# Short matmuls set between long ones in a TensorE-bound attention and gMLP kernel, and a last output tile cut 384 + 128

## The chip, the cores and the metric

The kernel runs on one core of a Trainium2 chip. The metric is the device time of one execution in microseconds; the time of a version is the median over its runs. Five engines work side by side, each through its own list of instructions in order: TensorE (PE; its weight loads are shown apart as PEld), VectorE (DVE), ScalarE (ACT), GpSimd (POOL) and SyncE (SP), which here only issues transfers.

## The reference

Two branches share the input x of 2048 rows by 512 columns, and a sigmoid gate per row mixes them.

```python
g = sigmoid((x * gate_w).sum(-1, keepdims=True))
# a: linear attention, 32 heads of 16
q, k, v = split(x @ wqkv)
phi(p) = concat(softmax(p @ w_phi), softmax(-(p @ w_phi)))      # 32 features per head
kv = einsum('bhsf,bhsd->bhfd', phi(k), v);  z = phi(k).sum over s
a = ((phi(q) @ kv) / (phi(q) . z + 1e-6)) @ wo
# b: gMLP
h = gelu(x @ w_in)                                              # 512 -> 1376
z1, z2 = h[:, :688], layernorm(h[:, 688:])
b = (z1 * (w_sp @ z2 + b_sp)) @ w_out                           # w_sp is 2048 x 2048
out = g * a + (1 - g) * b
```

All inputs are bfloat16. The product `w_sp @ z2` mixes along the rows and is the largest piece of work.

## The kernel before

Rows are cut into 16 tiles of 128. The order on each engine is written out by hand: the sequence in which the Python code calls its helpers is the sequence on every engine. All sums lie in one PSUM tile `ps` with 8 banks of 512 columns.

First come, per row tile, the input product of the gMLP (`z_piece`, L180), GELU on ACT, layer norm on DVE, and the value product (`v_proj`, L282). In between, `fold` multiplies the feature map into the key and query weights.

Then the loop at L516 runs 16 steps. Each step i has

- a spatial half tile `gg_half` (L396): 16 products of 344 columns that accumulate in bank 0 or 1. Two half tiles make one row tile of `w_sp @ z2`. When a half is done, DVE computes `u` from it (L404); after the second half, SP issues the transpose of `u` and the load of the spatial weights eight tiles on;
- `k_norm(i)`: DVE sums (L338) and inverts (L340), and then scales half of the key features, groups 0 to 3, while GpSimd scales groups 4 to 7 (L342);
- `kv_acc(i - 2)` (L372), the key sums: eight products of 65 columns, one per group of four heads, with a weight load each. They accumulate over all tiles in banks 3 and 4, called `slots`;
- `k_proj(i + 2)`: four products of 512 columns (L327), then two exponentials on ACT (L333). In three of the steps a query tile is projected, and another half tile and the query's `q_norm` follow.

Two more half tiles, the key sums of tiles 14 and 15 and `kv_extract` (DVE, L379 and L384) stand between this loop and the next.

The loop at L535 runs 16 steps j over the query tiles. Eleven half tiles are left; `gg_at` says which steps have one (step 2 has two, and steps 4, 6, 8, 10, 12 and 15 none). Each step has these half tiles, then `q_num(j)`: the query sums, eight products of 68 columns into `slots` (L420), which need the transposed query features of the tile (a transfer issued by `q_norm` three steps before, L364) and the release of `slots` by DVE, which reads them in `rd` (L424) and `o` (L426); SP then issues the transpose of `o` (L433). Then `q_proj(j + 4)`, `q_norm(j + 3)` and `out_tile(j - 3)`: 6 products for the gMLP (L439) and 4 for the attention (L444), a copy by ACT (L448) and the store (L449). The last output tile, 15, is made in two parts of 256 columns in banks 6 and 7, the first stored from SP's queue, the second from ACT's.

Of the kernel before, what the change touches and what calls it, by code (L numbers as in the profile page):

```python
# [14 lines left out]
P = 128  # L15
S = 2048
D = 512
# [5 lines left out]
NT = S // P  # L23
NDT = D // P
# [6 lines left out]
NHG = 8  # L31
HW = 4 * DH
VP = HW + 2
QW = HW + 4
# [5 lines left out]
def kernel(  # L40
# [14 lines left out]
    nc = tc.nc  # L55
# [9 lines left out]
    ps = psp.tile([P, 8, CH], FP32, name="ps")  # L65
# [5 lines left out]
    xT = pers.tile([P, NDT, S], BF16, name="xT")  # L71
    w_in = pers.tile([P, NDT, F + 1], BF16, name="w_in")
    wv = pers.tile([P, NDT, D], BF16, name="wv")
    wq = pers.tile([P, NDT, D], BF16, name="wq")
    wk = pers.tile([P, NDT, D], BF16, name="wk")
# [4 lines left out]
    vv = pers.tile([P, NT, NHG, VP], BF16, name="vv")  # L80
    wsp = pers.tile([P, WSLOTS, NT, P], BF16, name="wsp")
    kvx = pers.tile([P, NHG, QW], BF16, name="kvx")
# [59 lines left out]
    def load_wsp(t):  # L142
        nc.sync.dma_start_transpose(
            out=wsp[:, t % WSLOTS, :, :], in_=B_w_sp[t * P:(t + 1) * P, :]
        )
# [166 lines left out]
    KBANK = (2, 6)  # L312
    QBANK = (5, 7)
    ek_t = {}
    eq_t = {}
    w_in_flat = w_in[:].rearrange("p d f -> p (d f)")

    def e_slot(i):
        if i == 5:
            flat = xn[:].rearrange("p t d -> p (t d)")  # L320
        else:
            flat = w_in_flat[:, i * 2 * D:(i + 1) * 2 * D]
        return flat.rearrange("p (g a n) -> p g a n", g=NHG, a=2)

    def feat(t, w, b, e):
        for dt in range(NDT):
            nc.tensor.matmul(  # L327
                ps[:, b, :], lhsT=xT[:, dt, t * P:(t + 1) * P], rhs=w[:, dt, :],
                start=(dt == 0), stop=(dt == NDT - 1),
            )  # L330
        src = ps[:, b, :].rearrange("p (g n) -> p g n", g=NHG)
        for a, sc in enumerate((1.0, -1.0)):
            nc.scalar.activation(out=e[:, :, a, :], in_=src, func=AF.Exp, scale=sc)  # L333
# [12 lines left out]

    def k_proj(t):
        ek_t[t] = e_slot(t % 4)
        feat(t, wk, KBANK[t % 2], ek_t[t])

    def k_norm(t):
        norm(ek_t[t])

    def q_proj(t):
        eq_t[t] = e_slot(4 + t % 2 if t < 4 else (t - 4) % 6)
        feat(t, wq, QBANK[t % 2], eq_t[t])

    eT_t = {}

    def q_norm(t):  # L360
        e = eq_t.pop(t)
        norm(e)
        eT = wqkT[:, 2 * (t % 4):2 * (t % 4) + 2, :].rearrange("p a (b n) -> p (a b) n", n=P)
        nc.sync.dma_start_transpose(out=eT, in_=e.rearrange("p g a n -> p (g a n)"))  # L364
        eT_t[t] = eT

    slots = ps[:, 3:5, :].rearrange("p b (c w) -> p (b c) w", w=P)

    def kv_acc(t):
        ek = ek_t.pop(t)  # L370
        for g in range(NHG):
            nc.tensor.matmul(  # L372
                slots[:, g, 0:HW + 1], lhsT=ek[:, g, :, :].rearrange("p a n -> p (a n)"),
                rhs=vv[:, t, g, 0:HW + 1],
                start=(t == 0 and g % 4 == 0), stop=(t == NT - 1), skip_group_check=True,
            )

    def kv_extract():
        nc.vector.tensor_tensor(  # L379
# [9 lines left out]

    uT_t = {}  # L390

    def gg_half(i, s0=0, s1=NT):
        tt, h = divmod(i, 2)
        b = i % 2
        for s in range(s0, s1):
            nc.tensor.matmul(  # L396
                ps[:, b, 0:HF], lhsT=wsp[:, tt % WSLOTS, s, :],
                rhs=zz[:, s, FH + h * HF:FH + (h + 1) * HF],
                start=(s == 0), stop=(s == NT - 1),
            )  # L400
        if s1 < NT:
            return
        u = upad[tt % 3]
        nc.vector.scalar_tensor_tensor(  # L404
            out=u[:, h * HF:(h + 1) * HF], in0=ps[:, b, 0:HF], scalar=bcol[:, tt:tt + 1],
            in1=zz[:, tt, h * HF:(h + 1) * HF], op0=ALU.add, op1=ALU.mult,
        )
        if h == 1:
            uT = uTpool.tile([P, NFT, P], BF16, name="uT")
            nc.sync.dma_start_transpose(out=uT[:, :, :], in_=u[:, :])  # L410
            uT_t[tt] = uT
            if tt + WSLOTS < NT:
                load_wsp(tt + WSLOTS)

    oT_t = {}

    def q_num(t):
        eT = eT_t.pop(t)
        for g in range(NHG):
            nc.tensor.matmul(  # L420
                slots[:, g, 0:QW], lhsT=eT[:, g, :], rhs=kvx[:, g, :], start=True, stop=True
            )
        rd = ring2.tile([P, NHG, 4], FP32, name="rd")
        nc.vector.reciprocal(out=rd[:], in_=slots[:, :, HW:QW])  # L424
        o = ring2.tile([P, D], BF16, name="o")
        nc.vector.scalar_tensor_tensor(  # L426
            out=o[:].rearrange("p (g h d) -> p g h d", g=NHG, h=4),
            in0=slots[:, :, 0:HW].rearrange("p g (h d) -> p g h d", h=4),
            scalar=gate[:, t:t + 1],
            in1=rd[:, :, :, None].to_broadcast([P, NHG, 4, DH]), op0=ALU.mult, op1=ALU.mult,  # L430
        )
        oT = oTpool.tile([P, NDT, P], BF16, name="oT")
        nc.sync.dma_start_transpose(out=oT[:, :, :], in_=o[:, :])  # L433
        oT_t[t] = oT

    def out_part(t, b, n0, n1, ob, dma):
        uT, oT = uT_t[t], oT_t[t]
        for ft in range(NFT):
            nc.tensor.matmul(  # L439
                ps[:, b, n0:n1], lhsT=uT[:, ft, :], rhs=w_out[:, ft, n0:n1],  # L440
                start=(ft == 0), stop=False,
            )
        for g in range(NDT):
            nc.tensor.matmul(  # L444
                ps[:, b, n0:n1], lhsT=oT[:, g, :], rhs=wo[:, g, n0:n1],
                start=False, stop=(g == NDT - 1),
            )
        nc.scalar.activation(out=ob[:, n0:n1], in_=ps[:, b, n0:n1], func=AF.Copy)  # L448
        dma.dma_start(out=out2[t * P:(t + 1) * P, n0:n1], in_=ob[:, n0:n1])  # L449

    def out_tile(t):
        ob = ring3.tile([P, D], BF16, name="ob")
        if t < NT - 1:
            out_part(t, (2, 6)[t % 2], 0, D, ob, nc.scalar)
        else:
            out_part(t, 6, 0, D // 2, ob, nc.sync)
            out_part(t, 7, D // 2, D, ob, nc.scalar)

    uTpool = ctx.enter_context(tc.tile_pool(name="uTp", bufs=NT))
    oTpool = ctx.enter_context(tc.tile_pool(name="oTp", bufs=LAG + 2))  # L460
# [39 lines left out]
    for t in range(NT - VLAG, NT):  # L500
        v_proj(t)
    k_proj(0)
    k_proj(1)
    for t in range(NT - 5, NT):
        z1_gate(t)

    gg_next = 0

    def gg(n):
        nonlocal gg_next  # L510
        for _ in range(n):
            gg_half(gg_next)
            gg_next += 1

    Q_AT = {7: 0, 9: 1, 11: 2}
    for i in range(NT):  # L516
        gg(1)
        k_norm(i)
        if i >= 2:
            kv_acc(i - 2)  # L520
        if i + 2 < NT:
            k_proj(i + 2)
        if i in Q_AT:
            q_proj(Q_AT[i])
        if i - 1 in Q_AT:
            gg(1)
            q_norm(Q_AT[i - 1])

    q_proj(3)
    gg(2)  # L530
    kv_acc(NT - 2)
    kv_acc(NT - 1)
    kv_extract()
    gg_at = {0: 1, 1: 1, 2: 2, 3: 1, 5: 1, 7: 1, 9: 1, 11: 1, 13: 1, 14: 1}
    for j in range(NT):  # L535
        gg(gg_at.get(j, 0))
        q_num(j)
        if j + 4 < NT:
            q_proj(j + 4)
        if j + 3 < NT:  # L540
            q_norm(j + 3)
        if j >= LAG:
            out_tile(j - LAG)
    for j in range(NT - LAG, NT):
        out_tile(j)
# [28 lines left out]
```

## Time and profile before

| | |
|---|---|
| median of 3 runs | 208.38 us (208.34 to 208.63) |
| profiled execution | 208.87 us, its span 207.1 us |
| granted TensorE clock | 1.000 over the span |
| spatial products, L396, 344 columns | 512, busy 79.1 us |
| key sums, L372, 65 columns | 128, busy 6.5 us |
| query sums, L420, 68 columns | 128, busy 6.7 us |
| last copy by ACT (256 columns) | 204.21 us, 0.38 us long |
| last store issued | 204.62 us, landing after 1.5 us |

The span runs from the first to the last instruction of the profiled execution; its time also has what lies around the span. The rows of the timeline give the start in us, the duration, the engine, the line of the kernel, the operation with its tiles and shapes and, behind an x, how many follow each other without another group between. The duration of a matmul, about 0.19 us for a short one and 0.31 for a spatial one, contains a modelled tail in which the next ones already run; what a matmul takes from its engine is the distance to the next one's start.

### The profile page before, as it was taken

The numbers are of one execution on the slowest core, as the hardware profiler recorded it, in microseconds if no ns is written. First come the engines' busy times: TensorE is split into PE (matmuls) and PEld (weight loads), VectorE is DVE, ScalarE is ACT, GpSimd is POOL, SyncE is SP. The second block draws the span as 40 slices with busy tenths as digits, with TensorE's granted clock in tenths as the row PEclk, the third lists the DMA queues.
The fourth block names the chain that finished last, engine by engine and source line by source line (L and its number), as shares of the span: only waits on it lengthen the run. The fifth ranks groups of instructions, "written<-read, shape, count | busy, mean of one in ns | idle before, by whom it ended". The sixth has DMA issues, their size and how long they took to land.

```text
span 207.1 us, 3685 instructions
## 1 busy us (share of the span) xinstructions
PE 202.6 (98%) x1399; PEld 118.2 (57%) x1399; DVE 148.5 (72%) x304; ACT 82.1 (40%) x145; POOL 49.5 (24%) x46
## 2 busy tenths in 40 slices
PE   8899999999999999999999999999999999999994
PEld 7454555555455666666666667666455555555543
DVE  1048858376887988878888996698989778795500
ACT  3266757575684424250505102222524243341122
POOL 4000000000002343525352544032522252322000
DMA  6999899997000634472757771137765963567451
GB/s 188 233 188 255 178 178 227 173 188 234 0 3 0 138 69 112 101 127 67 162 118 112 139 170 41 38 90 76 170 140 119 151 162 80 134 135 164 101 104 51
DMA packets 90378, 26.50 MB, mean 128 GB/s; under 512 B 84168, under 2 KB 90360, under 8 KB 90360
## 3 DMA queue, kind: packets, MB, share of 16 engines
q1 hardware_dynamic: 87360, 23.84, 58.9%
q10 hardware_dynamic: 3000, 2.43, 3.9%
q8 instruction: 11, 0.18, 0.4%
q14 instruction: 7, 0.06, 0.1%
HBM read 3.44 MB, written 2.10 MB: 27 GB/s over the span
## 4 chain that ended last, share of the span: by engine, by line
PE 98%; issue 0%; ACT 0%; DVE 0%
PE ps L396 36%; PE ps L180 18%; PE ps L327 13%; PE ps L439 10%; PE ps L444 7%; PE ps L282 7%; PE ps L420 2%; PE ps L372 2%; PE ps L189 1%; PE ps L305 1%; PE ps L195 0%; ACT ob L448 0%; DVE w_in L212 0%; PE ps L209 0%
## 5 line engine op out<-in xcount | busy, mean ns | idle before, releaser
L396 PE MATMUL ps<-zz,wsp 128*128 128x344 bf16 x512 | 79.1, 310 | 0.0
L342 POOL TENSOR_TENSOR w_in<-w_in,rs 128x512 bf16<-128x512 bf16 x28 | 41.3, 1475 | 124.8 <-DVE rs L340 117.3
L396 PEld LDWEIGHTS <-wsp 128*128 128x128 bf16 x512 | 49.9, 98 | 27.9
L333 ACT ACTIVATE w_in<-ps 128x512 bf16<-128x512 f32 x56 | 30.1, 596 | 63.5 <-issue 21.5
L180 PE MATMUL ps<-w_in,xT 128*128 128x512 bf16 (+2 forms) x200 | 39.8, 350 | 0.7 <-DVE w_in L212 0.7
L338 DVE TENSOR_REDUCE zs<-w_in 128x64 f32<-128x1024 bf16 x28 | 33.8, 1209 | 0.0
L404 DVE SCALAR_TENSOR_TENSOR u<-ps,bcol,zz 128x344 bf16<-128x344 f32 x32 | 18.4, 574 | 18.6 <-PE ps L396 18.5
L180 PEld LDWEIGHTS <-xT 128*128 128x128 bf16 x200 | 18.9, 97 | 18.5 <-DMA w_in<-in_B_w_in_dram 1.0
L215 ACT ACTIVATE zz<-ps 128x1376 bf16<-128x1376 f32 (+2 forms) x18 | 21.4, 1190 | 18.9 <-PE ps L180 18.8
L439 PE MATMUL ps<-w_out,uT 128*128 128x512 bf16 (+1 forms) x102 | 23.5, 367 | 0.0
L224 DVE BATCH_NORM_STATS2 stats<-zz 128x6 f32<-128x344 bf16 x32 | 14.8, 505 | 11.2 <-ACT zz L215 11.2
L342 DVE TENSOR_TENSOR w_in<-w_in,rs 128x512 bf16<-128x512 bf16 x28 | 19.4, 692 | 1.0
L340 DVE RECIPROCAL rs<-zs 128x64 f32<-128x64 f32 x32 | 17.7, 552 | 3.2
L448 ACT ACTIVATE ob<-ps 128x512 bf16<-128x512 f32 (+1 forms) x17 | 9.7, 572 | 25.2 <-PE ps L444 23.7
L444 PE MATMUL ps<-wo,oT 128*128 128x512 bf16 (+1 forms) x68 | 16.6, 367 | 0.0
L327 PE MATMUL ps<-wq,xT 128*128 128x512 bf16 x64 | 16.4, 379 | 0.0
L327 PE MATMUL ps<-wk,xT 128*128 128x512 bf16 x64 | 16.2, 379 | 0.0
L327 PEld LDWEIGHTS <-xT 128*128 128x128 bf16 x128 | 10.8, 97 | 9.0
L282 PE MATMUL ps<-wv,xT 128*128 128x512 bf16 x64 | 15.6, 380 | 0.0
L439 PEld LDWEIGHTS <-uT 128*128 128x128 bf16 x102 | 9.7, 98 | 10.0
L426 DVE SCALAR_TENSOR_TENSOR o<-ps,st,rd 128x512 bf16<-128x512 f32 x16 | 12.0, 751 | 0.6
L444 PEld LDWEIGHTS <-oT 128*128 128x128 bf16 x68 | 6.7, 98 | 7.2
(56 smaller groups left out, 119.2 us busy)
## 6 DMA issues: line engine op xcount, KB each, us to landing
out_dram<-ob ACTq DMA_DIRECT2D x15, 128.0 KB, 1.9
w_out<-in_B_w_out_dram SPq DMA_DIRECT2D x1, 640.0 KB, 5.0
w_in<-in_B_w_in_dram SPq DMA_DIRECT2D x2, 256.0 KB, 4.1
wv<-in_A_wqkv_dram SPq DMA_DIRECT2D x1, 512.0 KB, 5.0
wo<-in_A_wo_dram SPq DMA_DIRECT2D x1, 512.0 KB, 5.4
w_in<-in_B_w_in_dram SPq DMA_DIRECT2D x1, 352.0 KB, 5.2
w_in<-in_B_w_in_dram ACTq DMA_DIRECT2D x2, 128.0 KB, 3.9
w_in<-in_B_w_in_dram SPq DMA_DIRECT2D x2, 128.0 KB, 3.5
```

The lines of the kernel that those rows point to most:

```text
L180: nc.tensor.matmul(zb[:, n0:n1], lhsT=xT[:, dt, t * P:(t + 1) * P], rhs=w_in[:, dt, n0:n1], start=(dt == 0), stop=(dt == NDT - 1),)
L215: nc.scalar.activation(out=zz[:, t, n0:n1], in_=zbank(t)[:, n0:n1], func=AF.Gelu_apprx_tanh)
L282: nc.tensor.matmul(ps[:, b, :], lhsT=xT[:, dt, t * P:(t + 1) * P], rhs=wv[:, dt, :], start=(dt == 0), stop=(dt == NDT - 1),)
L327: nc.tensor.matmul(ps[:, b, :], lhsT=xT[:, dt, t * P:(t + 1) * P], rhs=w[:, dt, :], start=(dt == 0), stop=(dt == NDT - 1),)
L333: nc.scalar.activation(out=e[:, :, a, :], in_=src, func=AF.Exp, scale=sc)
L338: nc.vector.tensor_reduce(out=zs[:], in_=ev, axis=AX.X, op=ALU.add)
L340: nc.vector.reciprocal(out=rs[:], in_=zs[:])
L342: eng.tensor_tensor(out=ev[:, sl, :], in0=ev[:, sl, :], in1=rs[:, sl, None].to_broadcast([P, H, DH]), op=ALU.mult,)
L396: nc.tensor.matmul(ps[:, b, 0:HF], lhsT=wsp[:, tt % WSLOTS, s, :], rhs=zz[:, s, FH + h * HF:FH + (h + 1) * HF], start=(s == 0), stop=(s == ...
L404: nc.vector.scalar_tensor_tensor(out=u[:, h * HF:(h + 1) * HF], in0=ps[:, b, 0:HF], scalar=bcol[:, tt:tt + 1], in1=zz[:, tt, h * HF:(h + 1 ...
L439: nc.tensor.matmul(ps[:, b, n0:n1], lhsT=uT[:, ft, :], rhs=w_out[:, ft, n0:n1], start=(ft == 0), stop=False,)
L444: nc.tensor.matmul(ps[:, b, n0:n1], lhsT=oT[:, g, :], rhs=wo[:, g, n0:n1], start=False, stop=(g == NDT - 1),)
```

## The change

`gg_half` takes a list `short` of up to eight calls. Behind each of its last eight products (s = 8 to 15) it issues one of them, so that long and short products alternate and a short one stands last. `DVE`'s `u` and all else that follows the half tile stay where they were in the list.

- Key sums: in steps 2 to 15 of the first loop the eight products of `kv_acc(i - 2)` are given to the step's first half tile; those of tile 14 to the second of the two half tiles behind the loop. Tile 15's stay a group of eight.
- Query sums: in the steps j of the second loop that have a half tile, except step 0, the eight products are given to the step's last half tile. In the other steps they stay a group of eight.
- Last output tile: parts of 384 and 128 columns instead of 256 and 256.

The rest of the diff splits helpers (`feat` into `feat_mm` and `feat_exp`, `kv_mm` and `q_mm` for single products), which leaves the order of instructions as it was.

```diff
+    def kv_mm(t, g):
+        nc.tensor.matmul(
+            slots[:, g, 0:HW + 1], lhsT=ek_t[t][:, g, :, :].rearrange("p a n -> p (a n)"),
+            rhs=vv[:, t, g, 0:HW + 1],
+            start=(t == 0 and g % 4 == 0), stop=(t == NT - 1), skip_group_check=True,
+        )
...
-    def gg_half(i, s0=0, s1=NT):
+    def gg_half(i, short=()):
         tt, h = divmod(i, 2)
         b = i % 2
-        for s in range(s0, s1):
+        for s in range(NT):
             nc.tensor.matmul(
                 ps[:, b, 0:HF], lhsT=wsp[:, tt % WSLOTS, s, :],
                 rhs=zz[:, s, FH + h * HF:FH + (h + 1) * HF],
                 start=(s == 0), stop=(s == NT - 1),
             )
-        if s1 < NT:
-            return
+            if s >= NT - len(short):
+                short[s - NT]()
...
+    def q_mm(t, g):
+        nc.tensor.matmul(
+            slots[:, g, 0:QW], lhsT=eT_t[t][:, g, :], rhs=kvx[:, g, :], start=True, stop=True
+        )
...
-            out_part(t, 6, 0, D // 2, ob, nc.sync)
-            out_part(t, 7, D // 2, D, ob, nc.scalar)
+            out_part(t, 6, 0, D - P, ob, nc.sync)
+            out_part(t, 7, D - P, D, ob, nc.scalar)
...
-    def gg(n):
+    def gg(n, short=()):
         nonlocal gg_next
-        for _ in range(n):
-            gg_half(gg_next)
+        for k in range(n):
+            gg_half(gg_next, short if k == n - 1 else ())
             gg_next += 1
+
+    def kv_short(t):
+        return [lambda g=g: kv_mm(t, g) for g in range(NHG)]
...
     for i in range(NT):
-        gg(1)
+        gg(1, kv_short(i - 2) if i >= 2 else ())
         k_norm(i)
-        if i >= 2:
-            kv_acc(i - 2)
...
     q_proj(3)
-    gg(2)
-    kv_acc(NT - 2)
+    gg(2, kv_short(NT - 2))
     kv_acc(NT - 1)
...
     for j in range(NT):
-        gg(gg_at.get(j, 0))
+        short = [lambda g=g: q_mm(j, g) for g in range(NHG)]
+        if 0 < j and j in gg_at:
+            gg(gg_at[j], short)
+        else:
+            gg(gg_at.get(j, 0))
+            for mm in short:
+                mm()
         q_num(j)
```

More of the change, by code (lines that the diff above doesn't have):

```diff
@@ L323, in e_slot, with feat_mm, feat_exp @@
         return flat.rearrange("p (g a n) -> p g a n", g=NHG, a=2)
[L325 to L330, printed above, removed]
+    def feat_mm(t, w, b, dt):
+        nc.tensor.matmul(
+            ps[:, b, :], lhsT=xT[:, dt, t * P:(t + 1) * P], rhs=w[:, dt, :],
+            start=(dt == 0), stop=(dt == NDT - 1),
+        )
+    def feat_exp(b, e):
         src = ps[:, b, :].rearrange("p (g n) -> p g n", g=NHG)
@@ L348, in k_proj @@
         ek_t[t] = e_slot(t % 4)
-        feat(t, wk, KBANK[t % 2], ek_t[t])
+        b = KBANK[t % 2]
+        for dt in range(NDT):
+            feat_mm(t, wk, b, dt)
+        feat_exp(b, ek_t[t])
     def k_norm(t):
@@ L355, in q_proj @@
         eq_t[t] = e_slot(4 + t % 2 if t < 4 else (t - 4) % 6)
-        feat(t, wq, QBANK[t % 2], eq_t[t])
+        b = QBANK[t % 2]
+        for dt in range(NDT):
+            feat_mm(t, wq, b, dt)
+        feat_exp(b, eq_t[t])
     eT_t = {}
@@ L367 @@
     slots = ps[:, 3:5, :].rearrange("p b (c w) -> p (b c) w", w=P)
+    def kv_mm(t, g):
[4 more added lines that the diff above has]
+        )
     def kv_acc(t):
-        ek = ek_t.pop(t)
         for g in range(NHG):
[L372 to L376, printed above, removed]
+            kv_mm(t, g)
     def kv_extract():
@@ L415 @@
     oT_t = {}
+    def q_mm(t, g):
+        nc.tensor.matmul(
+            slots[:, g, 0:QW], lhsT=eT_t[t][:, g, :], rhs=kvx[:, g, :], start=True, stop=True
+        )
     def q_num(t):
[L418 to L422, printed above, removed]
         rd = ring2.tile([P, NHG, 4], FP32, name="rd")
```

## The prediction

> **What bounds the kernel now.** I read the page's busy times first, then the chain that ended last, then TensorE's waits, and then single stretches of the timeline around the short products.
>
> ```profile
> PE 202.6 (98%) x1399; PEld 118.2 (57%) x1399; DVE 148.5 (72%) x304; ACT 82.1 (40%) x145; POOL 49.5 (24%) x46
> ...
> PE 98%; issue 0%; ACT 0%; DVE 0%
> ```
>
> TensorE is busy for 98% of the span, and the chain that ended last lies on it for 98%. So a time saved between two matmuls is saved at the end, as long as no new wait appears. TensorE's waits are two in all, both in the first 10 us:
>
> ```profile
> PE ps L189 <- PEq L558: 0.8, 1, 0.8
> PE ps L180 <- DVE w_in L212: 0.7, 1, 0.7
> ```
>
> What the change can win is therefore in how closely matmuls follow each other. The timeline of TensorE around two groups of short products (start, duration, and how many; a matmul's duration contains a modelled tail, so I read starts):
>
> ```profile
> 120.47 0.42 PE L372 MATMUL ps<-vv,w_in 128*128 128x65 bf16 x8
> ...
> 120.73 1.62 PE L396 MATMUL ps<-zz,wsp 128*128 128x344 bf16 x10
> ```
>
> ```profile
> 128.84 0.67 PE L372 MATMUL ps<-vv,w_in 128*128 128x65 bf16 x16
> 129.35 2.50 PE L396 MATMUL ps<-zz,wsp 128*128 128x344 bf16 x16
> 131.69 0.42 PE L420 MATMUL ps<-kvx,wqkT 128*128 128x68 bf16 x8
> 131.94 1.02 PE L327 MATMUL ps<-wq,xT 128*128 128x512 bf16 x4
> ```
>
> Sixteen key products take 129.35 - 128.84 = 0.51 us, 32 ns each; eight take 0.26 us; eight query products take 0.25 us. The single starts in the trace, to the nanosecond, give 256.1 ns for a group of eight key products (mean of 14 groups) and 256.6 ns for query products (16 groups): 32.0 and 32.1 ns each. Compare what a product's columns need. Sixteen products of 344 columns: (2.50 - 0.31)/15 = 146 ns from start to start, 0.31 being one's duration; the single starts give 145.8, and 215.7 for 512 columns, 55.7 for 128. That is a line of 0.417 ns per column plus 2.5 ns: 29.6 ns for 65 columns, 30.8 for 68. The shorts in a group thus run some 2 ns above their columns. The first of a group doesn't: from its start to the second's it is 29.2 ns (key) and 30.2 (query) in the mean. Its successor's weight load starts 1 ns after it. So the pace of the group is that of weight loads, one per 32 ns, and a short that comes after a long product escapes it for one slot.
>
> **The change, part by part.**
>
> Key shorts. In steps 2 to 15 (14 groups) and in the pair of half tiles behind the loop (1 group) the eight shorts move into the last eight products of a half tile: 120 shorts, each with a 344-column product ahead of it. I price each at the first slot's 29.2 instead of 32.0: 120 x 2.8 = 0.34 us saved. By the fitted line (29.6) it would be 0.29.
>
> Query shorts. Steps 1, 2, 3, 5, 7, 9, 11, 13, 14: 9 x 8 = 72 shorts, 30.2 instead of 32.1: 72 x 1.9 = 0.14 us saved (0.09 by the line). Steps 0, 4, 6, 8, 10, 12, 15 stay as they are. Together 0.48 us.
>
> That alternation as such isn't in the trace, so both ends: no gain is the one end (a short costs its 32 ns wherever it stands, because its 3 ns of credit are paid back by the next). The end below nothing is the second slot of a group, which is 34.5 ns (key) and 35.6 (query): if each isolated short cost that, 120 x 2.5 + 72 x 3.5 = 0.55 us lost. I take the first slot, because it is exactly the situation of the change: long product before, weights loaded long ago, next load starting with the short. The long product behind a group (512 columns at L327) starts on time and takes 215 ns, no more than elsewhere.
>
> The Trainium skill (TensorE: Matmul & The Clock Gate, "The mechanism" under "Packing small matmuls") says that a weight load overlaps a running matmul only when the two use different row groups. By that, order would change nothing, and only the tail term below would be left, 208.26. The trace disagrees: the loads at L396 last 98 ns, begin 1 to 2 ns after a matmul's start, and the pace is still 145.8 ns.
>
> Waits that come earlier, each by eight longs less one (the first short follows the ninth product, 9 x 0.146 = 1.31 us after the half tile's start). I cost all at nothing. Behind a waiting short stand the other seven long products and everything after them, and DVE's `u` waits for these. So the cover matters:
> Key shorts need the weights normalised by DVE (groups 0 to 3) and GpSimd (4 to 7). The tightest is step 15, tile 13:
>
> ```profile
> 120.28 0.69 DVE L342 TENSOR_TENSOR w_in<-w_in,rs 128x512 bf16<-128x512 bf16 x1
> ...
> 120.39 1.50 POOL L342 TENSOR_TENSOR w_in<-w_in,rs 128x512 bf16<-128x512 bf16 x1 [1.50 <-DVE rs L340]
> ```
>
> DVE's half ends at 120.97 and the first short would start at 120.73 + 1.31 = 122.04; GpSimd's ends at 121.89 and its first short, four pairs later (0.70), at 122.74. Cover 1.07 and 0.85 us.
> Query shorts need DVE to have read the previous tile's sums (`o`, L426) and the transposed tile, whose transfer (L364) was issued over 5 us before. `o` moves too: the last long product starts 7 x 0.03 = 0.21 us later, so `u` and, behind it on DVE, `rd` and `o` do. Step 3 is the tightest of the moved ones:
>
> ```profile
> 142.00 0.75 DVE L426 SCALAR_TENSOR_TENSOR o<-ps,st,rd 128x512 bf16<-128x512 f32 x1
> ```
>
> It ends at 142.75, with the shift 142.96; the first short comes at 142.04 + 1.31 = 143.35: cover 0.39 us. Step 15 is not moved, but its `o` of step 14 is late by 0.21: 193.76 + 0.75 + 0.21 = 194.72 against the shorts at 195.10: cover 0.38. Step 1 has 134.11 against 133.51, 0.60. The one release of TensorE by DVE in the trace (gate column, L212) took 0.05 us from DVE's end to the matmul. If the cover went, each of these would cost what DVE is late beyond 0.3.
> The queues: no transfer is moved past another. On SP the transposes of `u` and `o` start up to 0.21 us later, with the reload of the spatial weights behind `u`; `o` is used three tiles later, `u` later still, the reload 14 half tiles later. Key exponentials on ACT that reuse a slot come no earlier than before. The later `u` delays the key normalisation by up to 0.21 us, which the covers above hold.
>
> Last tile. 10 products of 384 columns (162.5 ns by the line) and 10 of 128 (55.7) take 2.18 us, as 20 of 256 do (109). So TensorE ends at the same time, and ACT's last copy is shorter:
>
> ```profile
> 204.21 0.38 ACT L448 ACTIVATE ob<-ps 128x256 bf16<-128x256 f32 x1 [0.71 <-PE ps L444]
> 204.62 0.34 ACTq L449 DMA_DIRECT2D out_dram<-ob  x1
> ```
>
> A copy of 512 columns takes 0.60, of 256 0.38, so 128 takes about 0.27 and 384 about 0.49 (estimates by the line through the two). The first copy would run from 203.66 to 204.15, out of the way of the second at 204.21, by 0.06. Gain 0.11 us. The transfer behind it lands 1.5 us after its issue whatever else happens; its packets fall from 512 to 256 bytes. The trace has 27 ns for 512 and 46 ns for 1024, hence about 17 for 256, eight per DMA engine: 0.08 us less at best. At worst a 256-byte packet costs as much as a 1024-byte one (0.15 more) and the larger first transfer, issued 0.66 later at 204.18, is still in the way (8 packets of about 37 ns, 0.15 of it overlapping). The tail lies between -0.19 and +0.19; I take -0.12, the copy and a little. The Trainium skill (DMA: Bandwidth & Descriptors, Specifications) puts the least size for full rate at 512 bytes, with a read-modify-write below; it speaks for the upper end, and by that end the forecast would be 208.1. No run here has such a packet.
>
> Sum: -0.34 - 0.14 - 0.12 = -0.60 us. The profiled execution took 208.87 us (span 207.1 and 1.77 around it), so 208.27 for such a one; it lay 0.49 above the median of 208.38, which I take as the base: 207.78.
>
> **The rivals.**
> Order does not matter: shorts cost 32 ns in any place, the first slot's credit is paid by the product behind. For it speaks that the first two slots of a group sum to 64 ns, twice 32. Against it, that the first slot follows the columns (one ns between 65 and 68). Time 208.38 - 0.12 = 208.26, the same as before.
> Slower: the weight load behind an isolated short is exposed, so that a short costs the second slot's 34.5 to 35.6 ns, at 192 places. It decides from 32 ns on: each ns above costs 0.19 us. Price 0.55, less the tail: 208.38 + 0.55 - 0.12 = 208.8. For it, that no load in this kernel has had to fit into 30 ns with a 344-column product behind it; against it, the 31 to 34 ns before a 512-column product at a group's end.
> A wait takes the place: DVE's `o` is later than I read at steps 3 and 15, by 0.2 us each past its cover, say: 207.78 + 0.4 = 208.2. Against it the covers of 0.38.
>
> **How the numbers follow.** 0.2% is 0.42 us, about what can be told from no change here: 207.96 and 208.80 are the bounds. The forecast as summed: 0.57, of which 0.51 ends as faster (a gain of 0.60, with 0.19 of tail and 0.1 between medians as its doubts) and 0.06 as the same. Order does not matter: 0.19, the same. A wait: 0.08, the same. Slower: 0.16, of it 0.13 past the bound and 0.03 within it. So faster 0.51, same 0.36, slower 0.13. The range reaches from 207.45 (0.60 and 0.19 of doubt in the tail and 0.14 between medians) to 208.5, which takes in the unchanged order and the wait; the forecast's own range is 207.45 to 208.0.
>
> **What would show it.** In the changed kernel's timeline, a half tile with shorts should take 16 x 146 + 8 x 29 to 30 ns, 2.57 us, with no wait at L372's and L420's successors; 2.59 says that order does not matter, 2.62 that loads are exposed. TensorE's waits should still be the two above. The last copy should take 0.27 and the last transfer land at about 1.5 us. I am wrong if any release by `o` appears among TensorE's waits, or if the alternating products are paced by something that groups of one kind don't show.

## The result and the profile after

The changed kernel takes 208.02 us in the median of 22 runs (207.61 to 208.32) against 208.33 us for the kernel before in as many; the ratio is 0.9984 with a 95% interval of 0.9977 to 0.9990. By the ratio that is 0.33 us less, 0.16%, with 0.21 to 0.48 us as the interval (the two medians lie 0.31 us apart): a real gain, below the 0.2% that I had called the least that can be told, and a little over half of the 0.60 us forecast.

The page of the changed kernel, busy times and the chain that ended last, and then TensorE's waits:

```profile
PE 202.3 (98%) x1399; PEld 117.8 (57%) x1399; DVE 148.5 (72%) x304; ACT 82.1 (40%) x145; POOL 49.5 (24%) x46
...
PE 96%; DMA 2%; SPq 0%; ACT 0%; issue 0%
```

```profile
PE ps L189 <- PEq L573: 0.8, 1, 0.8
PE ps L180 <- DMA w_in<-in_B_w_in_dram: 0.4, 1, 0.4
```

TensorE still carries the end, and it has two waits, both in the first 10 us, where nothing was changed. So none of the shorts waits for DVE, GpSimd or a transfer. A step's end in the changed kernel's timeline (TensorE alone):

```profile
109.73 0.19 PE L377 MATMUL ps<-vv,w_in 128*128 128x65 bf16 x1
109.76 0.31 PE L405 MATMUL ps<-zz,wsp 128*128 128x344 bf16 x1
109.91 0.19 PE L377 MATMUL ps<-vv,w_in 128*128 128x65 bf16 x1
109.94 0.31 PE L405 MATMUL ps<-zz,wsp 128*128 128x344 bf16 x1
110.08 0.19 PE L377 MATMUL ps<-vv,w_in 128*128 128x65 bf16 x1
...
110.99 0.38 PE L326 MATMUL ps<-wk,xT 128*128 128x512 bf16 x1
```

The first pair, short to short, takes 0.18 us and the second 0.17. By the single starts, a key short's slot is 29.2 ns in the mean (104 of them), as forecast, but the spatial product behind it does not always take 145.8: behind the first and the fifth key short of a group it takes 150.8 ns in the mean, 150 or 151 in each of the 15 groups. Eight key pairs (a spatial product and the short behind it) take 1409.4 ns together, and eight query pairs 1412.8. No group is more than 1 ns off, so no wait hides in one of them either.

The span's first instruction to its last is 206.4 us, 0.77 us less than before. That is more than the change did, and the start of the first spatial product tells why. The timeline of TensorE in the kernel before, at three marks (first half tile; half tile of step 0 and of step 14 of the second loop):

```profile
60.75 0.75 PE L396 MATMUL ps<-zz,wsp 128*128 128x344 bf16 x4
...
129.35 0.31 PE L396 MATMUL ps<-zz,wsp 128*128 128x344 bf16 x1
...
190.35 0.46 PE L396 MATMUL ps<-zz,wsp 128*128 128x344 bf16 x2
```

The same marks in the changed kernel:

```profile
60.36 1.04 PE L405 MATMUL ps<-zz,wsp 128*128 128x344 bf16 x6
...
128.81 0.89 PE L405 MATMUL ps<-zz,wsp 128*128 128x344 bf16 x5
...
189.74 1.04 PE L405 MATMUL ps<-zz,wsp 128*128 128x344 bf16 x6
```

0.38 us of the difference are there at the first mark, ahead of all that was changed. From that mark on the two differ by 0.16 us in the key stage (68.45 instead of 68.61), 0.07 in the query stage (60.93 for 61.00) and 0.16 from there to the end of the span (16.62 for 16.78): 0.39 us, inside the interval of the runs.

### The profile page after: what moved, and what is told of

Its sections match the earlier page's. It is cut to its first block, busy times and chain, and to the rows that moved or that the text cites. A ratio compares the mean times of both kernels' runs of the same rounds, so it can differ in the third digit from the quotient of the medians.

```text
span 206.4 us, 3685 instructions
## 1 busy us (share of the span) xinstructions
PE 202.3 (98%) x1399; PEld 117.8 (57%) x1399; DVE 148.5 (72%) x304; ACT 82.1 (40%) x145; POOL 49.5 (24%) x46
## 4 chain that ended last, share of the span: by engine, by line
PE 96%; DMA 2%; SPq 0%; ACT 0%; issue 0%
PE ps L405 36%; PE ps L180 18%; PE ps L326 13%; PE ps L448 10%; PE ps L453 7%; PE ps L282 7%; DMA w_in<-in_B_w_in_dram 2%; PE ps L427 2%; PE ps L377 2%; PE ps L305 1%; SPq L112 0%; SPq L108 0%; ACT ob L457 0%; PE ps L209 0%
## 5 line engine op out<-in xcount | busy, mean ns | idle before, releaser
L405 PE MATMUL ps<-zz,wsp 128*128 128x344 bf16 x512 | 84.1, 309 | 0.0
L448 PE MATMUL ps<-w_out,uT 128*128 128x512 bf16 (+2 forms) x102 | 23.5, 366 | 0.0
L377 PE MATMUL ps<-vv,w_in 128*128 128x65 bf16 x128 | 21.7, 193 | 0.0
L457 ACT ACTIVATE ob<-ps 128x512 bf16<-128x512 f32 (+2 forms) x17 | 9.7, 572 | 25.1 <-PE ps L453 19.9
L453 PE MATMUL ps<-wo,oT 128*128 128x512 bf16 (+2 forms) x68 | 16.6, 366 | 0.0
L427 PE MATMUL ps<-kvx,wqkT 128*128 128x68 bf16 x128 | 15.8, 194 | 0.0
```

The lines of the kernel that those rows point to most:

```text
L377: nc.tensor.matmul(slots[:, g, 0:HW + 1], lhsT=ek_t[t][:, g, :, :].rearrange("p a n -> p (a n)"), rhs=vv[:, t, g, 0:HW + 1], start=(t == 0 ...
L405: nc.tensor.matmul(ps[:, b, 0:HF], lhsT=wsp[:, tt % WSLOTS, s, :], rhs=zz[:, s, FH + h * HF:FH + (h + 1) * HF], start=(s == 0), stop=(s == ...
L427: nc.tensor.matmul(slots[:, g, 0:QW], lhsT=eT_t[t][:, g, :], rhs=kvx[:, g, :], start=True, stop=True)
L448: nc.tensor.matmul(ps[:, b, n0:n1], lhsT=uT[:, ft, :], rhs=w_out[:, ft, n0:n1], start=(ft == 0), stop=False,)
L453: nc.tensor.matmul(ps[:, b, n0:n1], lhsT=oT[:, g, :], rhs=wo[:, g, n0:n1], start=False, stop=(g == NDT - 1),)
```

## The experiments

**Each part alone.** Theory one: the shorts are worth less than forecast, the tail what was forecast. Theory two: the shorts are worth their 0.48 us and the tail takes some back.

Last tile alone, on the kernel before:

```diff
-            out_part(t, 6, 0, D // 2, ob, nc.sync)
-            out_part(t, 7, D // 2, D, ob, nc.scalar)
+            out_part(t, 6, 0, D - P, ob, nc.sync)
+            out_part(t, 7, D - P, D, ob, nc.scalar)
```

> The kernel before with only the last output tile cut 384 + 128; all short products stay in groups of eight. Theory one (the shorts are worth less than forecast, the tail what was forecast): 0.10 to 0.17 us less than before; last copy 0.28 us, last transfer 1.5 us, end of the span 3.02 us after the last matmul's start against 3.23, of which 0.05 is the shorter last matmul. Theory two (the shorts are worth the full 0.48 us, the small packets take some of it back): 0.1 to 0.2 us more than before.

All shorts, with the last tile as before (the diff above the other way, on the changed kernel):

> The changed kernel with the last tile cut 256 + 256 again. Theory one: 0.20 to 0.25 us less than before. Theory two: 0.48 us less. Theory three (order of the products does not matter): 0.0 us.

Key shorts alone, from the one before:

```diff
-        if 0 < j and j in gg_at:
+        if False:
```

> Only the key shorts alternate; query shorts in groups, last tile 256 + 256. Theory one: 15 groups save 10 to 11 ns each, 0.16 us less than before, with a spatial product of 151 ns behind the shorts of head groups 0 and 4. Theory two: 0.34 us less.

Query shorts alone, on the changed kernel with the last tile as before:

```diff
-        gg(1, kv_short(i - 2) if i >= 2 else ())
+        gg(1)
         k_norm(i)
+        if i >= 2:
+            kv_acc(i - 2)
...
-    gg(2, kv_short(NT - 2))
+    gg(2)
+    kv_acc(NT - 2)
```

> Only the query shorts alternate. Theory one: nine groups save 8 to 9 ns each, 0.07 to 0.09 us less than before, pairs of 176.7 ns. Theory two: 0.14 us less.

Ratios to the kernel before (11 or 12 runs each), and the stages of the profiled execution from mark to mark, in us:

| kernel | ratio (95%) | first mark at | key stage | query stage | to the end |
|---|---|---|---|---|---|
| before | 1 | 60.75 | 68.609 | 60.996 | 16.779 |
| last tile alone | 1.0003 (0.9994 to 1.0011) | 60.57 | 68.612 | 60.996 | 16.625 |
| all shorts, no tail | 0.9988 (0.9978 to 0.9999) | 60.59 | 68.451 | 60.928 | 16.769 |
| key shorts alone | 0.9996 (0.9986 to 1.0006) | 60.40 | 68.453 | 60.997 | 16.768 |
| query shorts alone | 0.9993 (0.9981 to 1.0004) | 60.77 | 68.612 | 60.928 | 16.772 |
| changed kernel | 0.9984 (0.9977 to 0.9990) | 60.36 | 68.451 | 60.929 | 16.618 |

By the stages each part does the same alone as with the others: key shorts -0.156 us, query shorts -0.068, the last tile -0.154. The query group of step 14 lies behind the third mark; like the eight others it should be worth about 0.008, but the last stage can't show that, since key shorts alone, which leave this group as it was, come out 0.011 shorter there. Theory two falls: its shorts would have shown 0.34 and 0.14. By time alone the parts can't be told from nothing, except all shorts together, 0.25 us (0.02 to 0.46). For the last tile the runs allow from 0.13 us less to 0.23 more, and the trace's 0.154 lies just outside; so its gain is shown by the profile, not by time. The profiles agree on it: the last stage takes 16.77 to 16.78 us in the five kernels here that have the last tile 256 + 256 and their query shorts at 68 columns, and 16.62 to 16.64 in the seven that have it 384 + 128, a gain of 0.13 to 0.16.

The end of the last-tile kernel, where the trace has it (ACT, and the two queues that issue the stores):

```profile
203.47 0.83 ACT L448 ACTIVATE ob<-ps 128x384 bf16<-128x384 f32 x2 [1.03 <-PE ps L444]
...
203.99 0.37 SPq L449 DMA_DIRECT2D out_dram<-ob  x1
204.34 0.34 ACTq L449 DMA_DIRECT2D out_dram<-ob  x1
```

The two copies follow each other closely, the second 0.28 us long. From the last store's issue to the end is 2.46 us here (206.80 - 204.34) against 2.51 before (207.13 - 204.62). So 0.11 us come from the shorter copy and 0.05 from what follows the issue: the transfer lands after 1.50 us instead of 1.53, and the rest of the end is a little shorter too.

**What paces a group of shorts.** The prediction held weight loads responsible, one per 32 ns. If so, fewer columns leave a group as it is.

Fewer columns in groups, on the kernel before, and in alternation, on the changed kernel (the same edit to `kv_mm` and `q_mm` there):

```diff
-                slots[:, g, 0:HW + 1], lhsT=ek[:, g, :, :].rearrange("p a n -> p (a n)"),
-                rhs=vv[:, t, g, 0:HW + 1],
+                slots[:, g, 0:(32 if t else HW + 1)], lhsT=ek[:, g, :, :].rearrange("p a n -> p (a n)"),
+                rhs=vv[:, t, g, 0:(32 if t else HW + 1)],
...
-                slots[:, g, 0:QW], lhsT=eT[:, g, :], rhs=kvx[:, g, :], start=True, stop=True
+                slots[:, g, 0:(32 if t else QW)], lhsT=eT[:, g, :], rhs=kvx[:, g, 0:(32 if t else QW)], start=True, stop=True
```

> The kernel before with 32 columns in each short of tiles 1 to 15, in groups of eight; half of the key and query sums is left out. If the weight loads set the pace of a group, eight take 254 to 257 ns as with 65 and 68 columns. If something per column sets it, eight take 130 to 190 ns.

> The changed kernel with 32 columns in each short of tiles 1 to 15 instead of 65 or 68; half of the key and query sums is left out, so the output is not the reference's. If the weight load of the next long product needs its 28 to 30 ns behind a short, a short and a long take 174 to 176 ns together as now, 1400 to 1410 for eight pairs. If columns alone count, 145.8 + 15.8 = 161.6 ns, 1293 for eight.

A group in the kernel before with 32 columns (TensorE's timeline):

```profile
72.45 0.35 PE L372 MATMUL ps<-vv,w_in 128*128 128x32 bf16 x8
72.65 0.59 PE L327 MATMUL ps<-wk,xT 128*128 128x512 bf16 x2
```

Eight shorts with eight weight loads take 0.20 us; by the single starts 203 to 205 ns, 25.5 ns each, in both kinds. The weight loads' pace is therefore 25 ns or less, and not what held 65 columns at 32. In alternation (changed kernel, 32 columns):

```profile
109.55 0.18 PE L377 MATMUL ps<-vv,w_in 128*128 128x32 bf16 x1
109.58 0.31 PE L405 MATMUL ps<-zz,wsp 128*128 128x344 bf16 x1
109.72 0.18 PE L377 MATMUL ps<-vv,w_in 128*128 128x32 bf16 x1
109.75 0.31 PE L405 MATMUL ps<-zz,wsp 128*128 128x344 bf16 x1
109.89 0.18 PE L377 MATMUL ps<-vv,w_in 128*128 128x32 bf16 x1
```

Eight pairs take 1373 ns (key) and 1372 (query) in the mean, so 26 ns for a short over the 145.8 of its companion: no better than in a group. The 28 to 30 ns that I expected a load to need behind a short are not needed. With 32 columns alternation gains nothing.

The Trainium skill (TensorE: Matmul & The Clock Gate, "Wait — 56ns, not 53.3ns?") states that the distance between matmul starts does not fall below about 25 ns however few the columns. The 25.5 ns agree, here with a weight load to each matmul.

**From 16 to 112 columns.** One number per tile, in the key shorts, on the kernel before and on the changed kernel:

```diff
+    SCAN = {1: 16, 2: 24, 3: 32, 4: 40, 5: 48, 6: 56, 7: 60, 8: 64, 9: 66, 10: 72, 11: 80, 12: 96, 13: 112}
+    vflat = vv[:].rearrange("p t g v -> p (t g v)")
...
-                slots[:, g, 0:HW + 1], lhsT=ek[:, g, :, :].rearrange("p a n -> p (a n)"),
-                rhs=vv[:, t, g, 0:HW + 1],
+                slots[:, g, 0:SCAN.get(t, HW + 1)], lhsT=ek[:, g, :, :].rearrange("p a n -> p (a n)"),
+                rhs=vflat[:, (t * NHG + g) * VP:(t * NHG + g) * VP + SCAN.get(t, HW + 1)],
```

> The kernel before with another number of columns in the key shorts of each tile: 16, 24, 32, 40, 48, 56, 60, 64, 66, 72, 80, 96, 112 in tiles 1 to 13 (65 in tiles 0, 14, 15); below 65 part of the key sums is left out, above 66 columns are computed that nobody reads. Groups of eight. Theory P (a load cannot follow a load faster than 32 ns while columns stream, 25 when few do): the pace steps from 25 to 32 ns somewhere between 32 and 64 columns, stays at 32 up to 71 and then follows the column line (72: 32.5, 80: 35.8, 96: 42.5, 112: 49.2). Theory Q (a fixed extra of 2 ns on the column line with a floor of 25): 48: 25, 56: 27.8, 64: 31.2, 72: 34.5, 80: 37.8, 96: 44.5, 112: 51.2.

> The changed kernel with the same numbers of columns per tile, the shorts alternating with spatial products. If alternation frees a short from everything but its columns, eight pairs take 8 x 145.8 plus eight times the column line (64: 1400, 72: 1427, 80: 1453, 96: 1507, 112: 1560), with the floor of 25.7 ns for 16 to 48 columns (1372). If the extra of 6 ns per group (1409 against 1403 at 65 columns) stems from the load, it is gone from 80 columns on, where a load has time; if from PSUM, it stays.

Two groups of the first kernel, 60 and 72 columns:

```profile
95.68 0.38 PE L374 MATMUL ps<-vv,w_in 128*128 128x60 bf16 x8
95.90 0.38 PE L327 MATMUL ps<-wk,xT 128*128 128x512 bf16 x1
```

```profile
110.05 0.44 PE L374 MATMUL ps<-vv,w_in 128*128 128x72 bf16 x8
110.33 0.38 PE L327 MATMUL ps<-wk,xT 128*128 128x512 bf16 x1
```

Single starts, eight shorts in ns; for alternation the eight pairs less 8 x 145.8; the column line is the prediction's, 0.417 ns per column and 2.5. Each number is from a single group of eight, except for 65 columns, where they are the means of the kernel before and of the changed kernel. Single groups of equal code differ by up to 5 ns (254 to 259 at 65 columns), so smaller differences say nothing. (At 112 columns a record is missing in both traces; they are left out.)

| columns | 16 to 48 | 56 | 60 | 64 | 65 | 66 | 72 | 80 | 96 |
|---|---|---|---|---|---|---|---|---|---|
| group | 203 to 205 | 210 | 221 | 244 | 256 | 257 | 280 | 298 | 342 |
| alternation | 204 to 209 | 210 | 222 | 237 | 243 | 242 | 265 | 291 | 340 |
| column line | (below the floor) | 207 | 220 | 233 | 237 | 240 | 260 | 287 | 340 |

Both theories fall: P would have 256 at 64 and 60 columns or a step to it, and then the plain line at 72; Q's constant extra is missing at 60 and at 96. What a group pays above its columns is 11 to 20 ns, from 64 to 80 columns alone; at 60 and at 96 it is on the line within the scatter, and up to 48 columns it stays at a floor of 25.5 ns each. Alternation takes away most of that extra (7 of 11 ns at 64 columns, 13 of 19 at 65, 15 of 17 at 66, 15 of 20 at 72, 7 of 11 at 80) and there is nothing to take elsewhere. At 64 and at 80 columns the 7 ns rest on one group each and are little more than the scatter. Why the extra sits between 64 and 80 columns these runs don't say.

**The two products of 151 ns.** Three edits to the changed kernel. One column more in each key short:

```diff
-            slots[:, g, 0:HW + 1], lhsT=ek_t[t][:, g, :, :].rearrange("p a n -> p (a n)"),
-            rhs=vv[:, t, g, 0:HW + 1],
+            slots[:, g, 0:VP], lhsT=ek_t[t][:, g, :, :].rearrange("p a n -> p (a n)"),
+            rhs=vv[:, t, g, 0:VP],
```

> The changed kernel with 66 instead of 65 columns in each key short (the 66th is a second column of ones that nobody reads). Theory A, the odd number of columns makes the 151 ns behind head groups 0 and 4: all spatial products fall to 146 or 147 ns and eight pairs take 1406 ns. Theory B, the change of PSUM bank (group 0 and group 4 are the first ones in banks 3 and 4) makes them: they stay, eight pairs take 1412 to 1413 ns.

Another order, (0, 4, 1, 5, 2, 6, 3, 7) and (0, 1, 4, 5, 2, 3, 6, 7):

```diff
-        return [lambda g=g: kv_mm(t, g) for g in range(NHG)]
+        return [lambda g=g: kv_mm(t, g) for g in (0, 4, 1, 5, 2, 6, 3, 7)]
```

> The changed kernel with the alternating key shorts in the order 0, 4, 1, 5, 2, 6, 3, 7, so that each goes to the other PSUM bank than the one before it. Theory B (change of bank): all eight spatial products that follow a short take 151 ns, eight pairs 1435 to 1440 ns. Theory C (something in head groups 0 and 4 themselves, their address): two in a row, behind the first and the second short, take 151 ns, the others 146; eight pairs 1409 to 1410 ns as in the changed kernel. Theory A says nothing on the place.

> The changed kernel with the key shorts in the order 0, 1, 4, 5, 2, 3, 6, 7: the PSUM bank changes behind every second short. If a change of bank makes the 151 ns, they stand behind the first, third, fifth and seventh short (1418 to 1425 ns for eight pairs); if only the first short in each bank does, behind the first and the third (1409); if the place in the group does, behind the first and the fifth (1409).

No accumulation:

```diff
-            start=(t == 0 and g % 4 == 0), stop=(t == NT - 1), skip_group_check=True,
+            start=True, stop=True, skip_group_check=True,
```

> The changed kernel with every key short starting its own sum instead of adding to what PSUM holds, so that only the last tile's key sums are left. If adding in a PSUM bank that was not touched since the last step makes the two 151 ns in a group, they are gone and eight pairs take 1404 to 1406 ns, paired evenly as the query shorts are; if not, 1409 as in the changed kernel.

| kernel | eight key pairs, ns | spatial products of 150 to 152 ns |
|---|---|---|
| changed kernel | 1409.4 | behind the first and fifth short |
| 66 columns | 1409.5 | the same |
| no accumulation | 1409 to 1411 | the same |
| order 0, 4, 1, 5, 2, 6, 3, 7 | 1407.6 | behind the first only |
| order 0, 1, 4, 5, 2, 3, 6, 7 | 1407.9 | behind the first, in 2 of 15 groups behind the third too |

In the traces without accumulation and of the last order a record is missing in one group each; its total is left out.

An odd number of columns is out (the 66th costs nothing), and so is adding in PSUM. A change of bank as such is out too: with one at every short there is one slow product and not eight. The head group alone is out for the second one: behind group 4 in its new place the product takes 145 ns in the one order, and 145 to 147 in 13 of 15 groups of the other; in two it takes 151 and 152, for a reason that I don't know. For the first one the head group and the place were not told apart, since group 0 comes first in every order. What makes them stays open; the scan has them from 64 to 80 columns, there behind other places too, and not at 60 or 96, so they belong to the same extra. Either order gains about 0.026 us more in the key stage (68.424 and 68.426 us): by the stages the best versions here, by a step that the runs' times could not show.

## Why the prediction was right or wrong

- **What bounds the kernel**: right. Between the marks every nanosecond saved on TensorE is at the end of the stage.
- **Waits that come earlier, costed at nothing**: right, with no wait of TensorE on DVE, GpSimd or a transfer in the stages changed. The cover that I read as 0.39 us at step 3 is there. DVE in the changed kernel:

```profile
141.67 0.75 DVE L435 SCALAR_TENSOR_TENSOR o<-ps,st,rd 128x512 bf16<-128x512 f32 x1
```

and TensorE at that step:

```profile
142.79 0.19 PE L427 MATMUL ps<-kvx,wqkT 128*128 128x68 bf16 x1
```

  `o` ends at 142.42 and the first short starts at 142.79: 0.37 us.
- **The price of an isolated short** is the step that failed. "So the pace of the group is that of weight loads, one per 32 ns, and a short that comes after a long product escapes it for one slot" was wrong in its cause: with 32 columns loads follow each other at 25 ns. And the first slot was the wrong row to price by, because the product behind was charged nothing for it ("The long product behind a group starts on time and takes 215 ns, no more than elsewhere"). Eight key shorts did take 8 x 29.2 ns as priced, 22.5 less than the 256.1 of a group; but the spatial products between them took 9.4 ns more together (1409.4 - 8 x 29.2 - 8 x 145.8), and the product behind the group 1.5 more (216.6 ns for 215.1 before). That leaves 11.6 of the 22.5; the key stage as a whole shows 10.5 per group. In alternation a query short takes 30.0 ns, which is below the column line, and the product behind it 146.7 instead of 145.8, so the pair is at 176.6 in the mean, which is the line (30.8 + 145.8). I had worked out that price, 0.09 us, beside the 0.14 that I took; the runs gave 0.08. For key shorts the line's 0.29 instead of 0.34 would still have been too much: the measured 0.16 has the two slow products per group in it (5 ns each, some of it won back by the next) and the 1.5 ns behind a group. A half tile with shorts takes 2.58 us, between the 2.57 named as the sign of the forecast and the 2.59 of an order that does not matter.
- **The last tile**: -0.15 us in the trace for -0.12 forecast, with the copy at 0.28 us (0.27 estimated) and the 256-byte packets at 17.6 ns each (17 estimated from 27 and 46). Of the 0.08 us that the small packets were to save at best, 0.03 came: the landing moved from 1.53 to 1.50 us. That the first copy would be out of the way by 0.06 us held (0.07). "No run here has such a packet" is true of stores alone: the profile's page of the kernel before counts 84168 packets under 512 bytes, nearly all 256 bytes long and on the queue of SP, which issues the transposes. The Trainium skill (DMA: Bandwidth & Descriptors, Specifications) has a read-modify-write below 512 bytes. The packets' times (17.6 ns for 256 bytes, 26.7 for 512, 35.8 for 768, 45.8 for 1024) lie on one line, and nothing of it shows in them.
- **The rivals**: "order does not matter" is refuted at 65 and 68 columns by the stages of the kernels with one part each, but it is true at 32, and about half of it was true here: the credit of the first slot is partly paid by the products behind. Exposed loads and new waits did not come.
- **The numbers**: 208.02 lies in the range, and just above the forecast's own (207.45 to 208.0). That says little, because the range was wide enough to hold the kernel before as well (208.33). "Faster by over 0.2%" had 0.51 and did not come; the gain ended in the case that had 0.36. The lower price, which I had in hand and set aside, is only a part of the reason: with it the sum is 0.29 + 0.09 + 0.12 = 0.50 us, which is still past the bound. The rest is what the key pairs cost above the line. From mark to mark the changed kernel gains 0.39 us of the 0.60: 0.16 of 0.34, 0.08 of 0.14, and 0.15 where 0.12 was forecast.

## What to carry to other kernels

Price a matmul that is moved between others by the pair, not by the distance from its start to the next start: what one start gains, the next can pay back. From 56 columns up, no eight pairs here came out more than 1 ns below the line over the columns of both. Before a pace is put down to weight loads, look at it with fewer columns: here 32 columns ran at 25 ns and 65 at 32, so the loads had not been the limit. And where an effect is a few tenths of a microsecond, compare stages between marks inside the trace; where the code was equal the key and query stages repeated to within 3 ns and the last one to within about 25, while whole executions spread over half a microsecond and more.

## What was not expected of the hardware

The first 60 us, which feed on transfers and were the same in all kernels, put the first spatial product anywhere from 59.80 to 60.77 us in 14 profiled executions; from there on the key and query stages of kernels with equal code agree to 3 ns, and the last stage, which ends with the stores, to about 25. The spread of the runs of one kernel (208.04 to 208.87 us) is of that size. And a group of short matmuls pays 1.4 to 2.5 ns each above its columns between 64 and 80 columns, while at 60 and at 96 it does not.
